# Sparse attention with two MLPs: thresholds moved to VectorE, v's product spread 2 and 3, the division in a job's fifth block

## The chip, the cores and the metric

The kernel runs on one core of a Trainium2 chip. The metric is the device time of one execution in microseconds, the median of three runs.

## The reference

Attention over 4 batches, 8 heads, 576 positions and 64 columns a head, followed by two MLPs over the 2304 tokens (512 to 2048 to 512 columns):

```python
scores = scale * np.matmul(q, k.transpose(0, 1, 3, 2))
thresh = np.max(scores, axis=-1, keepdims=True) - tau
scores = np.where(scores >= thresh, scores, -1000000000.0)
scores = scores - np.max(scores, axis=-1, keepdims=True)
attn = np.exp(scores)
attn = attn / (np.sum(attn, axis=-1, keepdims=True) + 1e-09)
attn_out = np.matmul(attn, v)
...
h = x @ w_in
g = np.where(h >= 1, h, np.where(h <= -1, 0.0, (h + 1) ** 2 / 4))
x = g @ w_out
...
h = x @ w_in
g = h * np.clip(h + 3.0, 0.0, 6.0) / 6.0
out = g @ w_out
```

All inputs and outputs are float32.

## The kernel before

The attention is cut into 16 jobs (a batch and a pair of heads), a job into five blocks of query rows: four of 128 rows for both heads, and a fifth that holds the last 64 rows of both. A block goes through these steps.

- Scores (`em_scores`, line 305): four matmuls on TensorE into the two halves of PSUM called P, one half for each head. A half is free again when its reader is done.
- Reduction (line 318): VectorE reads a head's scores, writes their negatives to `p` in SBUF and their row minimum to a column of `nm`. It is followed by a short readout of the accumulator.
- Exponential (`em_exp`, line 329): ScalarE makes `e` from `p` and `nm`, head by head.
- Threshold (line 333): GpSimd adds tau to both columns of `nm` at once and writes `th`.
- Mask (`em_mask`, line 339): VectorE compares `p` with `th`, multiplies by `e`, writes back to `p` and sums the rows into `z`.
- Transposes (`em_pt` and `em_tail`, line 263): TensorE turns `p`, one block later, four pieces for each head and one tail; ScalarE copies them to `Gf` and `Gt` (lines 363 and 377).
- The product with v (`pv_chunk`, line 399): each job has two groups of rows, a (blocks 1 and 2) and b (blocks 3 to 5), each of five chunks, a chunk being a matmul for each head.
- The division: `pre_norm` (lines 418, 419) adds 1e-9 to `z` and takes the reciprocal on VectorE, GpSimd spreads it (line 422), and `em_norm` (lines 436 to 445) transposes it on TensorE, multiplies on VectorE, stores x by SP's queue and starts loading v of the job after next.

`attention` writes this order down by hand, with a `yield` after each piece. Once the first four jobs are done, `mode["mlp"]` is set, and each `yield` gives the first MLP a credit of 0.57 pieces (`part1`, lines 602, 613 and 664), which take turns with the attention on TensorE. The weights of the MLPs are split into a high and a low part on ScalarE, VectorE and GpSimd (lines 116 to 142). A scheduler then sorts the instructions of each engine by its own simulated times and priorities, but within what `after` pins. `put` pins VectorE's attention work in the written order until `mode["mlp"]` is set.

In the attention alone a block has its products in two places, `pv_run(2)` after the first head's transposes and `pv_run(2)` at the end; beside the MLP it is `pv_run(3)` and `pv_run(2)`. There the division of a job stands in the third block of the next job; in the attention alone, in its fifth.

Of the kernel before, what the change touches and what calls it, by code (L numbers as in the profile page):

```python
# [18 lines left out]
def kernel(  # L19
# [185 lines left out]
    mode = {"mlp": False, "att": True, "step": False, "t": 0, "s": 0, "n": 0, "pin": True}  # L205
# [48 lines left out]
    last_on = {}  # L254

    def put(E, x):
        if mode["pin"] and E in "V":
            after(x, last_on.get(E))
        last_on[E] = x
        return x  # L260

    def turn(out, in_, pin):
        x = put("T", T.transpose(out, in_, ident))  # L263
        if pin:
            pe_pins.append(x)

    def unit_q(j):
        if j >= NJ or j in qt:
            return
        tm = unit_bank().rearrange("p e n -> p (e n)")  # L270
        for c in range(5):
            turn(tm[:, c * 128:(c + 1) * 128], qn[:, c, :], c == 0)
        load_q(j + 1)
        qt[j] = ap.tile([128, SEQ], F32, tag="qt", name="qt", bufs=2)
        reads(put("S", S.activation(out=qt[j], in_=tm[:, 0:SEQ], func=ACTF.Copy, scale=taus[:, 1:2])))

    def unit_k(j):

        if j >= NJ or j in kt:
            return  # L280
        tm = unit_bank().rearrange("p e n -> p (e n)")
        for i, c in enumerate((4, 0, 1, 2, 3, 4)):
            turn(tm[:, i * 128:(i + 1) * 128], kn[:, c, :], i == 0)
        load_k(j + 1)
        kt[j] = ap.tile([128, SEQ + TAIL], F32, tag="kt", name="kt", bufs=2)
        reads(put("S", S.activation(out=kt[j], in_=tm[:, 128 - TAIL:128 + MAIN + TAIL], func=ACTF.Copy)))
# [4 lines left out]
    def em_scores(j, i):  # L291

        last = i == NBLK - 1

        if not last:
            mode["s"] += 1
        ss = [unit_bank() for _ in range(1 if last else 2)]
        prev = None
        c = slice(i * 128, i * 128 + (TAIL if last else 128))
        for x, (h, e) in enumerate(((0, 0), (1, 1), (0, 1), (1, 0)) if last else ((0, 0), (1, 0), (0, 1), (1, 1))):  # L300
            r = slice(h * D, (h + 1) * D)
            k0 = e * HS + (TAIL if last or h == 0 else 0)
# [4 lines left out]
            prev = put("T", mm)  # L307
            if x == 0:
                pe_pins.append(mm)
                for y in range(1 if last else 2):  # L310
                    after(mm, readers.get((mode["s"] - y) % 2), True)
        nm = ap.tile([128, 2], F32, tag="nm", name="nm", bufs=3)
        th = ap.tile([128, 2], F32, tag="th", name="th", bufs=3)
        p = ap.tile([128, 2, 2, HS], F32, tag="p", name="p", bufs=3)
        if i == 0:
            zt[j] = ap.tile([128, 9], F32, tag="z", name="z", bufs=2)
        for x, s in enumerate(ss):
            reads(put("V", V.tensor_scalar(out=p[:, x], in0=s[:, :, 0:HS], scalar1=-1.0, scalar2=3e38,  # L318
                                           op0=ALU.mult, op1=ALU.min, accum_out=nm[:, x:x + 1])), len(ss) - 1 - x)
        blk[j, i] = (p, nm, th, [])  # L320
# [3 lines left out]
    def em_exp(j, i, x):  # L324
        p, nm, th, es = blk[j, i]
        if x >= (1 if i == NBLK - 1 else 2):
            return
        e = ap.tile([128, 2, HS], F32, tag="e", name="e", bufs=3)
        pins["S"] = put("S", S.activation(out=e, in_=p[:, x], func=ACTF.Exp, bias=nm[:, x:x + 1], scale=-1.0))  # L329
        es.append(e)  # L330
        if x == 0:
            n = 1 if i == NBLK - 1 else 2
            G.tensor_scalar(out=th[:, 0:n], in0=nm[:, 0:n], scalar1=taus[:, 0:1], scalar2=0.0, op0=ALU.add, op1=ALU.add)  # L333

    def em_mask(j, i):
        p, nm, th, es = blk.pop((j, i))
        for x, e in enumerate(es):
            z = ZCOL[x](i)
            put("V", V.scalar_tensor_tensor(out=p[:, x], in0=p[:, x], scalar=th[:, x:x + 1], in1=e,  # L339
                                            op0=ALU.is_le, op1=ALU.mult, accum_out=zt[j][:, z:z + 1]))  # L340
# [11 lines left out]
    def em_pt(j, i, h):  # L352
# [9 lines left out]
        if i < NBLK - 1:  # L362
            put("S", S.activation(out=f[:, h, :, d0:d0 + 128], in_=tm.rearrange("p (c n) -> p c n", c=4), func=ACTF.Copy))  # L363
        else:
            for x in HEADS:
                put("S", S.activation(out=f[:, x, :, d0:d0 + TAIL],
                                      in_=tm.rearrange("p (c h n) -> p h c n", c=4, h=2)[:, x], func=ACTF.Copy))

    def em_tail(j, i):
# [5 lines left out]
        if i < NBLK - 1:  # L375
            turn(tl[:, 0:128], p[:, MAIN:MAIN + 128], True)
            put("S", S.activation(out=t[:, d0:d0 + 128], in_=tl[:, 0:128], func=ACTF.Copy))
        else:
            turn(tl[0:TAIL, 0:128], p[:, MAIN:SEQ], True)
            for x in HEADS:  # L380
                put("S", S.activation(out=t[x * TAIL:(x + 1) * TAIL, d0:d0 + TAIL],
                                      in_=tl[0:TAIL, x * TAIL:(x + 1) * TAIL], func=ACTF.Copy))
# [3 lines left out]
    def pv_chunk():  # L386
# [10 lines left out]
        for h in (1, 0):  # L397
# [4 lines left out]
            prev = put("T", mm)  # L402
        if c == 4:
            del gt[g, j], o_t[j, g]
            put("S", S.activation(out=xu[j][:, d0:d0 + n], in_=o, func=ACTF.Copy))
# [7 lines left out]
    def pre_norm(j):  # L413
# [4 lines left out]
        put("V", V.tensor_scalar(out=z, in0=z, scalar1=1e-9, scalar2=None, op0=ALU.add))  # L418
        put("V", V.reciprocal(out=rz[:, :, 0], in_=z))
# [6 lines left out]
    def em_norm(j):  # L426
# [8 lines left out]
        for c in range(4):  # L435
            put("T", T.transpose(bm[:, c * 128:(c + 1) * 128], rb[:, c].rearrange("p h n -> p (h n)"), ident))
        bt = bm[:, 512:640]
        put("T", T.transpose(bt, rz[:, 4, :].to_broadcast([128, 128]), ident))
        x = xu.pop(j)
        put("V", V.tensor_tensor(out=x[:, 0:MAIN], in0=x[:, 0:MAIN], in1=bm[:, 0:MAIN], op=ALU.mult))  # L440
        if b < NB - 1:
            nc.sync.dma_start(out=xd[b][:, hp, :], in_=x[:, 0:MAIN])
        for h in HEADS:
            r = slice(64 * h, 64 * h + 64)
            reads(put("V", V.tensor_tensor(out=x[r, MAIN:SEQ], in0=x[r, MAIN:SEQ], in1=bt[r, 64 * h:64 * h + 64], op=ALU.mult)))
# [4 lines left out]
    def attention():  # L450
# [25 lines left out]
        for t in range(n + 6):  # L476
# [3 lines left out]
            if not mode["mlp"]:  # L480
                if t < n:
                    em_scores(j, i)
                    maskq.append((j, i))
                if t < n:
# [4 lines left out]
                yield  # L489
                now = due(1)  # L490
# [3 lines left out]
                pv_run(2)  # L494
                yield
# [4 lines left out]
                tails(1)  # L500
# [3 lines left out]
                pv_run(2)  # L504
# [12 lines left out]
            else:  # L517
# [24 lines left out]
                now = due(1)  # L542
# [319 lines left out]
    for _ in attention():  # L862
        if not mode["mlp"]:
# [9 lines left out]
            mode["pin"] = False  # L873
# [101 lines left out]
```

## Time and profile before

| | us |
|---|---|
| median of 3 runs | 1163.19 |
| lowest and highest | 1162.94 and 1165.3 |
| the profiled execution | 1165.27 |
| its span, first to last instruction | 1163.3 |

| engine | busy us | share of the span |
|---|---|---|
| TensorE (PE) | 1123.3 | 97% |
| VectorE (DVE) | 565.7 | 49% |
| ScalarE (ACT) | 627.6 | 54% |
| GpSimd (POOL) | 437.1 | 38% |

The shares are averages over stages that differ: the attention alone, the attention beside the MLP, and the two MLPs. The rows below are therefore taken by stage. A row of a group of instructions names the line, the engine, the operation, output and input; a row of the timeline begins with its start and its duration, and the bracket at its end tells how long the engine had been idle and what released it.

### The profile page before, as it was taken

Reading aid. Unit: us, or ns where it says so; the run is one execution under the profiler, and the core shown is the slowest. Engines: PE = TensorE matmul, PEld = TensorE weight load, DVE = VectorE, ACT = ScalarE, POOL = GpSimd, SP = SyncE. Lnnn points to the kernel's source line nnn. Section 1 sums busy time; section 2 is a strip of 40 time slices with the busy share of each in tenths; the row PEclk is TensorE's granted clock in tenths of the full one; section 3 lists DMA queues with packets and bytes.
Section 4 is the critical chain, followed back from the end, with each engine's and each line's share of the span. In section 5 each row is a group of like instructions: output and inputs, shape, how many; then the busy total and the mean of one; then the engine's idle time right before and its main releaser. Section 6 shows DMA issues by size and latency. Waiting matters only on the chain.

```text
span 1163.3 us, 17941 instructions
## 1 busy us (share of the span) xinstructions
PE 1123.3 (97%) x6680; PEld 900.7 (77%) x6680; DVE 565.7 (49%) x1128; ACT 627.6 (54%) x1234; POOL 437.1 (38%) x468
## 2 busy tenths in 40 slices
PE   7889888999999999999999999999999999999998
PEld 5455667677777777788889988888888888888886
DVE  4787886765564555624544756657631121121111
ACT  5676886766575656655665776645532222232222
POOL 1342675531121121215663765568722212222221
PEclk9999999999999999999999999999999999999999
DMA  6332434312112120002522345533110020010000
GB/s 165 89 89 61 119 93 134 103 50 69 37 47 52 43 52 22 11 11 92 154 73 89 106 142 156 179 109 109 55 59 1 1 68 1 1 46 1 19 1 37
DMA packets 105095, 79.82 MB, mean 69 GB/s; under 512 B 66352, under 2 KB 89904, under 8 KB 105008
## 3 DMA queue, kind: packets, MB, share of 16 engines
q1 hardware_dynamic: 103648, 78.38, 23.2%
q8 instruction: 53, 0.87, 0.3%
q10 hardware_dynamic: 1360, 0.30, 0.1%
q14 instruction: 34, 0.28, 0.1%
HBM read 61.34 MB, written 17.30 MB: 68 GB/s over the span
## 4 chain that ended last, share of the span: by engine, by line
PE 84%; DVE 8%; ACT 5%; issue 1%; POOL 1%; DMA 1%; ACTq 0%; DVEq 0%; POOLq 0%
PE Q L602 34%; PE P L644 27%; PE Q L664 7%; PE P L305 5%; PE Q L399 5%; PE Q L263 4%; DVE p L339 3%; DVE p L318 2%; ACT e L329 2%; ACT Gf L363 1%; PE P L263 1%; DVE w_c L133 1%; DVE xl L586 1%; DVE w_c L127 1%; POOL w_c L135 1%
## 5 line engine op out<-in xcount | busy, mean ns | idle before, releaser
L620 POOL TENSOR_TENSOR gl<-r,gh 128x512 fp32r<-128x512 f32 (+1 forms) x190 | 205.2, 1081 | 456.6 <-ACT gh L619 451.4
L602 PE MATMUL Q<-xh,wih 128*128 128x512 f32 (+1 forms) x760 | 264.4, 348 | 3.3 <-DVE r L613 3.2
L602 PE MATMUL Q<-xl,wih 128*128 128x512 f32 (+1 forms) x760 | 257.4, 339 | 0.0
L602 PE MATMUL Q<-xh,wil 128*128 128x512 f32 (+1 forms) x760 | 257.1, 338 | 0.0
L616 DVE SCALAR_TENSOR_TENSOR r<-r,Q 128x512 f32<-128x512 f32 (+1 forms) x80 | 50.7, 634 | 249.7 <-ACT r L615 249.6
L602 PEld LDWEIGHTS Q<-xh,wih 128*128 128x128 f32 x760 | 144.6, 190 | 33.7 <-issue 10.7
L619 ACT ACTIVATE gh<-r 128x512 fp32r<-128x512 f32 (+1 forms) x190 | 99.8, 526 | 122.1 <-PE P L644 52.7
L602 PEld LDWEIGHTS Q<-xl,wih 128*128 128x128 f32 x760 | 144.4, 190 | 16.1 <-issue 0.5
L602 PEld LDWEIGHTS Q<-xh,wil 128*128 128x128 f32 x760 | 144.2, 190 | 15.4
L339 DVE SCALAR_TENSOR_TENSOR p<-p,th,e 128x576 f32<-128x576 f32 x144 | 128.8, 911 | 42.4 <-POOL th L333 23.3
L318 DVE TENSOR_SCALAR_CACHE_REDUCE p<-P 128x576 f32<-128x576 f32 x144 | 103.6, 752 | 72.4 <-PE Q L263 50.8
L329 ACT ACTIVATE e<-p,nm 128x576 f32<-128x576 f32 x144 | 109.7, 774 | 49.5 <-DVE p L318 48.9
L615 ACT ACTIVATE r<-Q,three 128x512 f32<-128x512 f32 (+1 forms) x80 | 51.4, 643 | 144.2 <-PE Q L602 141.1
L263 PE MATMUL Q<-ident,p 128*128 128x128 f32 (+1 forms) x656 | 109.6, 282 | 16.1 <-DVE p L339 7.4
L613 DVE SCALAR_TENSOR_TENSOR r<-r,Q 128x256 f32<-128x256 f32 (+1 forms) x110 | 54.8, 499 | 121.9 <-ACT r L612 121.8
L263 PEld LDWEIGHTS Q<-ident,p 128*128 128x128 f32 (+1 forms) x656 | 72.8, 140 | 53.1 <-issue 12.2
L644 PE MATMUL P<-woh,gh 128*128 128x512 f32 x288 | 111.9, 390 | 0.6 <-DVE ob L702 0.6
L644 PE MATMUL P<-wol,gh 128*128 128x512 f32 x288 | 112.2, 390 | 0.0
L644 PE MATMUL P<-woh,gl 128*128 128x512 f32 x288 | 111.0, 390 | 0.0
L305 PE MATMUL P<-kt,qt 64*128 64x288 f32 (+1 forms) x640 | 99.2, 428 | 8.5 <-DVE p L318 6.7
L135 POOL TENSOR_TENSOR w_c<-w_c,w_raw 128x512 int32<-128x512 int32 x64 | 91.0, 1423 | 33.0 <-DVE w_c L133 23.9
L363 ACT ACTIVATE Gf<-Q 128x512 f32<-128x512 f32 x128 | 75.0, 591 | 39.7 <-PE Q L263 39.5
(85 smaller groups left out, 1873.5 us busy)
## 6 DMA issues: line engine op xcount, KB each, us to landing
w_raw<-in_moe_w_in_dram SPq DMA_DIRECT2D x32, 512.0 KB, 4.0
w_raw<-in_moe_w_out_dram SPq DMA_DIRECT2D x32, 512.0 KB, 3.7
kn<-in_k_dram SPq DMA_DIRECT2D x32, 128.0 KB, 2.6
vn<-in_v_dram SPq DMA_DIRECT2D x32, 128.0 KB, 2.8
x2p<-ob SPq DMA_DIRECT2D x16, 256.0 KB, 2.1
x2d<-ob SPq DMA_DIRECT2D x16, 256.0 KB, 3.5
xst<-x2d SPq DMA_DIRECT2D x16, 256.0 KB, 3.4
out_dram<-ob SPq DMA_DIRECT2D x16, 256.0 KB, 2.1
```

Of the source, the lines that this page charges most:

```text
L135: x = G.tensor_tensor(out=c.bitcast(I32), in0=c.bitcast(I32), in1=r, op=ALU.add)
L263: x = put("T", T.transpose(out, in_, ident))
L305: mm = T.matmul(o, qt[j][r, c], kt[j][r, k0:k0 + HS], start=True, stop=True, skip_group_check=True)
L318: reads(put("V", V.tensor_scalar(out=p[:, x], in0=s[:, :, 0:HS], scalar1=-1.0, scalar2=3e38, op0=ALU.mult, op1=ALU.min, accum_out=nm[:, x: ...
L329: pins["S"] = put("S", S.activation(out=e, in_=p[:, x], func=ACTF.Exp, bias=nm[:, x:x + 1], scale=-1.0))
L339: put("V", V.scalar_tensor_tensor(out=p[:, x], in0=p[:, x], scalar=th[:, x:x + 1], in1=e, op0=ALU.is_le, op1=ALU.mult, accum_out=zt[j][:, ...
L363: put("S", S.activation(out=f[:, h, :, d0:d0 + 128], in_=tm.rearrange("p (c n) -> p c n", c=4), func=ACTF.Copy))
L602: mm = T.matmul(h, l[:, kk * 128:(kk + 1) * 128], r, start=(x == 0), stop=(x == 3 * KD - 1))
L619: x = S.activation(out=gh, in_=r, func=ACTF.Copy)
L620: y = G.tensor_tensor(out=gl, in0=r, in1=f32(gh), op=ALU.subtract)
L644: T.matmul(a, l, r, start=(first and x == 0), stop=(last and x == 2))
L664: mm = T.matmul(o, l, r, start=(f == fs[0] and x == 0 and i == 0), stop=(f == fs[-1] and x == 2 and i == 1), skip_group_check=True)
```

## The change

The threshold becomes one small addition for each head, on VectorE instead of GpSimd. `put` and the pins of VectorE's order go. In the attention alone the products come as `pv_run(2)` right behind the scores and `pv_run(3)` at the end, the tail is turned ahead of the heads, and `pre_norm` stands between the two heads' transposes. Beside the MLP they come as `pv_run(2)` twice, `pre_norm` comes right behind the masks, and the division moves from the third block to the fifth. Where a `put(...)` is merely taken away, the diff is left out.

```diff
@@ em_exp
-        if x == 0:
-            n = 1 if i == NBLK - 1 else 2
-            G.tensor_scalar(out=th[:, 0:n], in0=nm[:, 0:n], scalar1=taus[:, 0:1], scalar2=0.0, op0=ALU.add, op1=ALU.add)
+        V.tensor_scalar(out=th[:, x:x + 1], in0=nm[:, x:x + 1], scalar1=taus[:, 0:1], scalar2=None, op0=ALU.add)
...
-    last_on = {}
-
-    def put(E, x):
-        if mode["pin"] and E in "V":
-            after(x, last_on.get(E))
-        last_on[E] = x
-        return x
...
@@ attention, alone
                     em_scores(j, i)
                     maskq.append((j, i))
+                pv_run(2)
+                yield
                 if t < n:
                     em_exp(j, i, 0)
                 if t < n:
                     em_exp(j, i, 1)
                 blocks_of("m", lag=0 if t < n else 0)
                 yield
+                tails(1)
                 now = due(1)
                 for b in now:
                     em_pt(*b, 0)
                     yield
-                pv_run(2)
-                yield
+                if i == 0 and 0 < j <= NJ:
+                    pre_norm(j - 1)
                 for b in now:
                     if b[1] < NBLK - 1:
                         em_pt(*b, 1)
                         yield
-                tails(1)
                 for b in now:
                     if b[1] in AFTER:
                         pvq.extend((b[0], AFTER[b[1]], c) for c in range(5))
-                pv_run(2)
+                pv_run(3)
+                if i == 4:
+                    unit_k(j + 1)
+                    yield
                 if i == 3:
                     unit_q(j + 1)
                     yield
-                if i == 4:
-                    unit_k(j + 1)
-                    yield
-                if i == 0 and 0 < j <= NJ:
-                    pre_norm(j - 1)
...
@@ attention, beside the MLP
                 blocks_of("m", lag=0 if t < n else 0)
+                if i == 0 and 0 < j <= NJ:
+                    pre_norm(j - 1)
                 yield
                 tails(2)
-                pv_run(3)
+                pv_run(2)
                 yield
-                if i == 0 and 0 < j <= NJ:
-                    pre_norm(j - 1)
-                if i == 2 and 0 < j <= NJ:
+                now = due(1)
+                if i == 4 and 0 < j <= NJ:
                     em_norm(j - 1)
                     done_jobs.add(j - 1)
                     yield
...
-                now = due(1)
```

The order of VectorE (DVE) in the first job, its third and fourth blocks (lines 318 and 310 are the reductions, 339 and 329 the masks, 323 the new thresholds). Before:

```order
L318 TENSOR_SCALAR p,nm<-P_239 128x576
L318 TENSOR_SCALAR p,nm<-P_240 128x576
L339 SCALAR_TENSOR_TENSOR p,z<-p,th,e 128x576 x2
L318 TENSOR_SCALAR p,nm<-P_288 128x576
L318 TENSOR_SCALAR p,nm<-P_289 128x576
L339 SCALAR_TENSOR_TENSOR p,z<-p,th,e 128x576 x2
```

With the change:

```order
L310 TENSOR_SCALAR p,nm<-P_241 128x576
L310 TENSOR_SCALAR p,nm<-P_242 128x576
L323 TENSOR_SCALAR th<-nm,taus 128x1 x2
L329 SCALAR_TENSOR_TENSOR p,z<-p,th,e 128x576
L310 TENSOR_SCALAR p,nm<-P_293 128x576
L329 SCALAR_TENSOR_TENSOR p,z<-p,th,e 128x576
L310 TENSOR_SCALAR p,nm<-P_294 128x576
L323 TENSOR_SCALAR th<-nm,taus 128x1 x2
L329 SCALAR_TENSOR_TENSOR p,z<-p,th,e 128x576 x2
```

The thresholds stand behind the reductions, and the fourth block's first reduction stands between the third block's two masks.

The order of TensorE (PE) in the third job's first two blocks (305 and 297 are the scores, 399 and 389 the products with v of the second job, 263 and 255 the transposes of p). Before, from the first block's last score on:

```order
L305 MATMUL P_640<-kt,qt 128x288
L399 MATMUL Q_675<-Gf,vn_97 64x320 x4
L305 MATMUL P_686<-kt,qt 128x288
L305 MATMUL P_687<-kt,qt 128x288
L305 MATMUL P_686<-kt,qt 128x288
L305 MATMUL P_687<-kt,qt 128x288
L263 MATMUL Q_706<-ident,p 128x128 x4
L399 MATMUL Q_675<-Gf,vn_97 64x320 x4
L263 MATMUL Q_716<-ident,p 128x128 x4
L263 MATMUL Q_722<-ident,p 128x128
L399 MATMUL Q_675<-Gt,vn_97 64x320 x2
```

With the change:

```order
L297 MATMUL P_648<-kt,qt 128x288
L389 MATMUL Q_690<-Gf,vn_97 64x320 x6
L297 MATMUL P_697<-kt,qt 128x288
L297 MATMUL P_698<-kt,qt 128x288
L297 MATMUL P_697<-kt,qt 128x288
L297 MATMUL P_698<-kt,qt 128x288
L389 MATMUL Q_690<-Gf,vn_97 64x320 x2
L389 MATMUL Q_690<-Gt,vn_97 64x320 x2
L255 MATMUL Q_726<-ident,p 128x128 x4
L255 MATMUL Q_723<-ident,p 128x128
L255 MATMUL Q_732<-ident,p 128x128 x4
```

Six products instead of four lie between the two blocks' scores, and the other four stand together ahead of the transposes; the tail stands between the two heads.

## Rows read from the trace of the kernel before

**Rows 1.** Busy time by stage: stretch, length, busy us (count) by engine, PEclk, DMA.

```profile
6.20:118.40 112.20, 96.51 (x672) 58.40 (x672) 82.26 (x210) 75.63 (x155) 32.45 (x53) 0.98 0.39 102
118.40:240.00 121.60, 107.33 (x770) 81.78 (x770) 95.63 (x200) 93.80 (x202) 76.44 (x85) 0.97 0.37 105
240.00:521.00 281.00, 277.38 (x2096) 216.38 (x2095) 148.56 (x392) 173.42 (x382) 51.81 (x96) 1.00 0.16 41
...
82.00:100.00 18.00, 14.59 (x102) 9.22 (x104) 13.87 (x32) 11.66 (x27) 9.23 (x10) 0.95 0.36 97
```

**Rows 2.** Waits of TensorE, 6.2 to 118.4: us in total, times, longest.

```profile
PE Q L263 <- DVE p L339: 7.4, 6, 1.6
PE P L305 <- DVE p L318: 5.8, 10, 1.5
```

**Rows 3.** Waits of VectorE, 6.2 to 118.4.

```profile
DVE p L339 <- POOL th L333: 10.6, 19, 1.3
...
DVE p L339 <- ACT e L329: 7.0, 9, 1.2
```

**Rows 4.** Timeline, 53 to 72 us: start, duration, instruction, idle time before it.

```profile
53.33 1.45 ACT L329 ACTIVATE e<-p,nm 128x576 f32<-128x576 f32 x2 [1.59 <-DVE p L318]
...
54.84 1.80 DVE L339 SCALAR_TENSOR_TENSOR p<-p,th,e 128x576 f32<-128x576 f32 x1 [0.93 <-POOL th L333]
...
58.26 0.75 DVE L318 TENSOR_SCALAR_CACHE_REDUCE p<-P 128x576 f32<-128x576 f32 x1
58.44 0.78 ACT L329 ACTIVATE e<-p,nm 128x576 f32<-128x576 f32 x1 [3.66 <-DVE p L318]
...
59.12 0.30 POOL L333 TENSOR_SCALAR th<-nm,taus 128x2 f32<-128x2 f32 x1 [0.46 <-DVE p L318]
...
59.45 0.82 DVE L339 SCALAR_TENSOR_TENSOR p<-p,th,e 128x576 f32<-128x576 f32 x1 [0.43 <-POOL th L333]
59.60 0.76 ACT L329 ACTIVATE e<-p,nm 128x576 f32<-128x576 f32 x1
...
60.39 0.82 DVE L339 SCALAR_TENSOR_TENSOR p<-p,th,e 128x576 f32<-128x576 f32 x1
...
70.73 0.77 ACT L329 ACTIVATE e<-p,nm 128x576 f32<-128x576 f32 x1
...
71.36 0.31 POOL L333 TENSOR_SCALAR th<-nm,taus 128x1 f32<-128x1 f32 x1
...
71.70 1.80 DVE L339 SCALAR_TENSOR_TENSOR p<-p,th,e 128x576 f32<-128x576 f32 x1 [1.27 <-POOL th L333]
```

**Rows 5.** Small additions on VectorE: timeline at the start, line 418's durations, its group.

```profile
3.73 0.15 DVE L818 TENSOR_SCALAR taus<-taus 128x1 f32<-128x1 f32 x1 [3.73 <-DMA taus<-in_tau_dram]
3.80 0.14 DVE L819 TENSOR_SCALAR taus<-taus 128x1 f32<-128x1 f32 x1
...
L418 DVE TENSOR_SCALAR z<-z x16: 158/172/1154, 33.9 to 499.6; 128x9 f32<-128x9 f32 x16
...
L418 DVE TENSOR_SCALAR z<-z 128x9 f32<-128x9 f32 x16 | 5.1, 318 | 0.3
```

**Rows 6.** Timeline of TensorE: scores, four products, nine transposes.

```profile
50.66 1.24 PE L305 MATMUL P<-kt,qt 64*128 64x288 f32 x8 [0.29 <-ACT kt L286]
...
51.83 1.30 PE L399 MATMUL Q<-Gf,vn 128*64 128x320 f32 x8
...
61.07 1.20 PE L263 MATMUL Q<-ident,p 128*128 128x128 f32 x9
```

**Rows 7.** 118.4 to 240: waits of masks for thresholds; busy time of the scores.

```profile
DVE p L339 <- POOL th L333: 2.0, 4, 0.6
...
118.40:240.00 121.60, 20.85 (x136) 11.06 (x136) 0.97 0.37 105
```

**Rows 8.** Timeline at 147 us: GpSimd and line 418.

```profile
146.70 1.82 POOL L135 TENSOR_TENSOR w_c<-w_c,w_raw 128x512 int32<-128x512 int32 x1
...
147.40 1.15 DVE L418 TENSOR_SCALAR z<-z 128x9 f32<-128x9 f32 x1
```

More of the change, by code (lines that the diff above doesn't have):

```diff
@@ L252, in reads @@
         readers[(mode["s"] - ago) % 2] = x
-    last_on = {}
-    def put(E, x):
-        if mode["pin"] and E in "V":
-            after(x, last_on.get(E))
-        last_on[E] = x
-        return x
     def turn(out, in_, pin):
-        x = put("T", T.transpose(out, in_, ident))
+        x = T.transpose(out, in_, ident)
         if pin:
@@ L274, in unit_q @@
         qt[j] = ap.tile([128, SEQ], F32, tag="qt", name="qt", bufs=2)
-        reads(put("S", S.activation(out=qt[j], in_=tm[:, 0:SEQ], func=ACTF.Copy, scale=taus[:, 1:2])))
+        reads(S.activation(out=qt[j], in_=tm[:, 0:SEQ], func=ACTF.Copy, scale=taus[:, 1:2]))
     def unit_k(j):
@@ L285, in unit_k @@
         kt[j] = ap.tile([128, SEQ + TAIL], F32, tag="kt", name="kt", bufs=2)
-        reads(put("S", S.activation(out=kt[j], in_=tm[:, 128 - TAIL:128 + MAIN + TAIL], func=ACTF.Copy)))
+        reads(S.activation(out=kt[j], in_=tm[:, 128 - TAIL:128 + MAIN + TAIL], func=ACTF.Copy))
     zt, gt, xu, p_t = {}, {}, {}, {}
@@ L306, in em_scores @@
             after(mm, prev)
-            prev = put("T", mm)
+            prev = mm
             if x == 0:
@@ L338, in em_mask @@
             z = ZCOL[x](i)
-            put("V", V.scalar_tensor_tensor(out=p[:, x], in0=p[:, x], scalar=th[:, x:x + 1], in1=e,
-                                            op0=ALU.is_le, op1=ALU.mult, accum_out=zt[j][:, z:z + 1]))
+            V.scalar_tensor_tensor(out=p[:, x], in0=p[:, x], scalar=th[:, x:x + 1], in1=e,
+                                            op0=ALU.is_le, op1=ALU.mult, accum_out=zt[j][:, z:z + 1])
         p_t[j, i] = p.rearrange("p h e n -> p (h e n)")
@@ L376, in em_tail @@
             turn(tl[:, 0:128], p[:, MAIN:MAIN + 128], True)
-            put("S", S.activation(out=t[:, d0:d0 + 128], in_=tl[:, 0:128], func=ACTF.Copy))
+            S.activation(out=t[:, d0:d0 + 128], in_=tl[:, 0:128], func=ACTF.Copy)
         else:
@@ L380, in em_tail @@
             for x in HEADS:
-                put("S", S.activation(out=t[x * TAIL:(x + 1) * TAIL, d0:d0 + TAIL],
-                                      in_=tl[0:TAIL, x * TAIL:(x + 1) * TAIL], func=ACTF.Copy))
+                S.activation(out=t[x * TAIL:(x + 1) * TAIL, d0:d0 + TAIL],
+                                      in_=tl[0:TAIL, x * TAIL:(x + 1) * TAIL], func=ACTF.Copy)
     o_t, pvq = {}, []
@@ L401, in pv_chunk @@
             after(mm, pe_pins[-1] if h else prev)
-            prev = put("T", mm)
+            prev = mm
         if c == 4:
             del gt[g, j], o_t[j, g]
-            put("S", S.activation(out=xu[j][:, d0:d0 + n], in_=o, func=ACTF.Copy))
+            S.activation(out=xu[j][:, d0:d0 + n], in_=o, func=ACTF.Copy)
     def pv_run(n):
@@ L417, in pre_norm @@
         rz = ap.tile([128, 9, 1], F32, tag="rz", name="rz", bufs=2)
-        put("V", V.tensor_scalar(out=z, in0=z, scalar1=1e-9, scalar2=None, op0=ALU.add))
-        put("V", V.reciprocal(out=rz[:, :, 0], in_=z))
+        V.tensor_scalar(out=z, in0=z, scalar1=1e-9, scalar2=None, op0=ALU.add)
+        V.reciprocal(out=rz[:, :, 0], in_=z)
         rb = ap.tile([128, 4, 2, 64], F32, tag="rb", name="rb")
@@ L444, in em_norm @@
             r = slice(64 * h, 64 * h + 64)
-            reads(put("V", V.tensor_tensor(out=x[r, MAIN:SEQ], in0=x[r, MAIN:SEQ], in1=bt[r, 64 * h:64 * h + 64], op=ALU.mult)))
+            reads(V.tensor_tensor(out=x[r, MAIN:SEQ], in0=x[r, MAIN:SEQ], in1=bt[r, 64 * h:64 * h + 64], op=ALU.mult))
         nc.sync.dma_start(out=xd[NB][:, hp, b * TAIL:(b + 1) * TAIL], in_=x[:, MAIN:SEQ])
```

21 lines of the change are left out of this document (10 added, 11 removed).

## The prediction

> **What bounds the kernel now.** I began with the busy times by stage [rows 1]. The reader should see three stages ahead of the pure MLP work. The attention alone (6.2 to 118.4 us) keeps TensorE busy 96.5 of 112.2 us. The attention beside the first weight splitting (118.4 to 240) keeps it busy 107.3 of 121.6. The rest of the attention (to 521) leaves 281.0 - 277.4 = 3.6 us idle, and after it come only the MLPs. The changed kernel issues the same matmuls, so it can only move idle time, 15.7 us in the first stage and 14.3 in the second, or the clock. [...]
>
> Then the waits of the first stage. TensorE waited 7.4 us for masks (line 339), 6 times, and 5.8 us for reductions (line 318), 10 times: 13.2 of its 15.7 us, on 16 occasions [rows 2]. The stage holds 25 blocks (five jobs, since the MLP begins when the first four are done, in the fifth job's last block), so VectorE's chain (reduction, threshold and exponential, mask) ends last in about 16 of 25. On VectorE the masks waited 10.6 us for GpSimd's threshold, 19 times, and 7.0 us for the exponential, 9 times [rows 3].
>
> **Thresholds on VectorE.** An ordinary block shows what the move is worth [rows 4]. The second reduction starts at 58.26 and takes 0.75, so it ends near 59.01. GpSimd's threshold runs from 59.12 to 59.42, and the mask starts at 59.45. The first head's exponential ran from 58.44 to 59.22. Without GpSimd the mask can start near 59.25. It gains 0.2 us and no more, because the exponential comes next. The same holds where GpSimd's queue made the wait long, at 71.70: the threshold ended at 71.67, the exponential at 71.50. Only at 54.84 was the exponential long done (two from 53.33 on in 1.45, the first by about 54.1), and there 0.7 us go. Together 18 x 0.2 + 0.7 = 4.3 us of VectorE's time.
>
> What it adds: no row has this operation inside a block. The nearest are two 128x1 operations at the start, 0.15 us long and 0.07 apart [rows 5], so a pair takes 0.07 + 0.15 = 0.22 us. It fits into the 0.2 us in which VectorE waits for the exponential anyway, which is its cover. With that cover gone it would cost 25 x 0.22 = 5.5 us in this stage, more than is saved. An addition on 128x9 has a median of 0.172 us but once took 1.154, and that dear end is taken up under the rivals. TensorE gets its share of what VectorE saves: 4.3 x 16/25 = **2.8 us**, between 0 and 4.3; I take it because the 128x1 rows are nearest in shape and they are short.
>
> **Nothing pinned.** In the new order 10 of the stage's 20 two-headed blocks have the next block's first reduction between their two masks (before, none). Where the second mask would wait for its exponential (7.0 / 9 = 0.78 us a time, in 9 of 20 blocks), the reduction fills the wait: 10 x 9/20 x 0.78 x 16/25 = 2.2 us at most. Against it, the second mask comes 0.83 us later (a reduction and a readout), and TensorE waited for a mask in 6 of 25 blocks: 10 x 6/25 x 0.83 = 2.0 us lost. I take **0**, between -2.0 and +2.2.
>
> **The products of v.** Four products take 1.30 us, a block's scores 1.24, its nine transposes 1.20 [rows 6]. In a job's first block TensorE has 1.24 + 1.30 = 2.5 us to do, in the second 1.24 + 6/4 x 1.30 + 1.20 = 4.4. VectorE's two reductions and two masks take 2 x 0.75 + 2 x 0.82 = 3.1 us and the waits. So the first block is VectorE's and the second TensorE's. In jobs 2, 3 and 4 one chunk (two products, 0.65 us) moves from the second to the first, which gains 3 x 0.65 = 1.95 us. In job 1 the opposite happens: all ten products lie in the second block, four more than before, which costs 1.30. Sum **0.65 us**, between -1.3 (the cost alone) and +2.0 (the gain alone). In the fourth blocks ten products now stand in a row between the transposes of the two heads. The next scores come no later by that, since the same ten lay in that block before.
>
> **The clock.** The dip costs 0.05 x 18.0 = 0.9 us [rows 1]. If the stops around it shrink it may go, if they grow there may be another. I take half, **0.45 us**, between -0.9 and +0.9.
>
> **The later stages.** From 118.4 to 240 there are 17 blocks (136 score records, 8 a block), and masks waited only 2.0 us for thresholds [rows 7]. VectorE, busy 95.6 of 121.6 us, gets 17 x 0.22 = 3.7 us more, and GpSimd, busy 76.4, loses its thresholds. I count 0, between +2.0 (those waits) and -3.7 (VectorE last throughout). The division moves to a job's fifth block, two blocks later, with its five transposes and three multiplications, which meet the transposes of k there. The MLP needs job 7's result after 240 products of line 602. The new order has exactly 240 ahead of that division (before, 228), so almost nothing queues behind it: 0. Were the MLP held up for the two blocks in each of the two batches that still follow, these four blocks would run as in the first stage, which idles 15.7 / 25 = 0.63 us a block: 2.5 us. On SP's queue the stores of x go out two blocks later, and so does v's next load, which is still several blocks ahead of its first use: 0. Past 240 us TensorE has 3.6 us idle to give, and a longer VectorE chain is covered by MLP matmuls: 0.
>
> **Sum.** 2.8 + 0 + 0.65 + 0.45 = 3.9 us. The profiled execution took 1165.27 us (its span is 1163.3), 2.08 above the median of 1163.19. Its own time becomes 1161.4, and the median, rounded, **1159** us.
>
> **Rivals.**
> *Slower: the threshold is caught behind GpSimd.* At 147.40 the 128x9 addition on VectorE took 1.15 us, while GpSimd's operation begun at 146.70 ran 1.82, to 148.52 [rows 8]. Both ended together. The addition's 16 cases average 0.318 us against the median of 0.172, so 0.146 more [rows 5]. If each block's pair pays that and the masks gain nothing, 25 + 17 blocks up to 240 us cost 42 x 0.146 = 6.1 us: **1169**. It decides from the point where a pair costs more than the 0.2 us of its cover. For it speaks that GpSimd is busy 76.4 of 121.6 us in the second stage. Against it, that the mask behind the threshold is caught by such operations already (1.80 instead of 0.82 at 54.84), so most of this wait is not new. Chance 0.20.
>
> [...]
>
> *No change.* The waits for the threshold become waits for the exponential, which queues on ScalarE behind the copies. In the block of rows 4 the second mask started at 60.39, just when its exponential (59.60 and 0.76) ended, and would do so again. Then the block's start moves but not its end, and the time stays at **1163**, within 2.3 us. Chance 0.24. That the change does nothing at all is excluded by the order, which moves all three engines' work.
>
> *More.* With all terms of the first stage at their upper ends, 4.3 + 2.2 + 2.0 + 0.9 = 9.4 us, and 2.0 from the second: 1163.2 - 11.4, or **1152**. [...] Chance 0.16.
>
> **How the numbers follow.** The forecast, from 1154 to 1160.9, has the remaining 0.40. A measurement of this kernel can tell about 0.2%, or 2.3 us, from no change. Faster: 0.40 + 0.16 = 0.56. Same: 0.24. Slower: 0.20. The range runs from all upper ends, 1152, to 1167, where two thirds of the slower case's price have been paid; what that case costs beyond, and the little below 1152, are under 0.2 together.
>
> **What would show it.** Right: no wait of a mask for GpSimd; waits for the exponential above 7.0 us; the first 25 blocks done about 4 us before 118.4; TensorE's idle time there near 12 us; thresholds near 0.15 us each. Wrong: thresholds of up to a microsecond, waits for masks above 7.4 us, TensorE idle well over 14.3 us in the second stage, or the lower clock in more stretches than before.

## The result, and the profile after

The changed kernel takes 1149.03 us (median of 4 runs, 1147.81 to 1149.29), the kernel before 1163.21 beside it: a ratio of 0.9872 (0.9855 to 0.9889). That is 14.2 us less where 4 were forecast, and 3 us below the range. The profiled executions are 17.3 us of span apart (1163.3 and 1146.0), since that of before lies 2.1 us above its median and that of after 1.2 below.

By stage, after (columns as in [rows 1]), with the stage of the MLPs alone as a fourth:

```profile
6.20:110.40 104.20, 91.19 (x676) 60.01 (x677) 87.93 (x257) 77.15 (x156) 24.70 (x28) 1.00 0.42 111
110.40:232.00 121.60, 112.35 (x826) 84.22 (x825) 104.23 (x245) 97.62 (x212) 71.16 (x71) 1.00 0.39 109
232.00:503.00 271.00, 270.07 (x2034) 208.44 (x2033) 147.92 (x444) 167.41 (x369) 37.55 (x55) 1.00 0.16 41
503.00:1146.00 643.00, 638.59 (x3133) 541.10 (x3132) 236.57 (x327) 283.37 (x498) 275.45 (x221) 1.00 0.22 68
```

The attention beside the MLP as one stretch, and what follows it, before:

```profile
118.40:520.40 402.00, 384.11 (x2859) 297.56 (x2860) 243.59 (x590) 266.61 (x581) 128.25 (x181) 0.99 0.22 60
...
520.40:1163.30 642.90, 638.62 (x3134) 541.01 (x3132) 239.60 (x328) 284.01 (x499) 274.75 (x221) 1.00 0.22 68
```

The attention alone is 8.0 us shorter (112.2 to 104.2), the attention beside the MLP 9.4 (402.0 to 121.6 + 271.0 = 392.6), the rest is unchanged. In the first stage TensorE's idle time fell by 2.7 us (15.7 to 13.0) and its busy time by 5.3. Beside the MLP idle time fell from 17.9 to 10.2 and busy time by 1.7. Much of the gain is thus busy time, which the prediction held to be fixed.

The waits of TensorE in the first stage, after, answer to [rows 2]:

```profile
PE P L297 <- DVE p L310: 5.4, 9, 1.5
PE Q L255 <- DVE p L329: 3.5, 4, 1.7
```

Those of VectorE there answer to [rows 3]:

```profile
DVE p L310 <- PE P L297: 10.6, 11, 4.1
DVE p L329 <- ACT e L321: 4.0, 7, 0.8
```

The threshold wait is gone (10.6 us before), waits for the exponential fell too (7.0 to 4.0), and the masks that TensorE waits for cost 3.5 us instead of 7.4. The new thresholds, and below them the 128x9 addition, after (minimum, median and longest in ns):

```profile
L323 DVE TENSOR_SCALAR th<-nm,taus x144: 199/207/216, 12.0 to 479.8; 128x1 f32<-128x1 f32 x144
...
L408 DVE TENSOR_SCALAR z<-z x16: 165/173/1164, 28.0 to 481.4; 128x9 f32<-128x9 f32 x16
```

Not one of the 144 thresholds was held up behind GpSimd, while the 128x9 addition still was, up to 1.16 us. In 19 of the 144 cases an operation of GpSimd that had begun earlier was still running, as here:

```profile
63.88 1.28 POOL L142 TENSOR_TENSOR wil<-w_c,wih 128x512 fp32r<-128x512 f32 x1
...
63.93 0.33 DVE L323 TENSOR_SCALAR th<-nm,taus 128x1 f32<-128x1 f32 x2
```

The pair ends 0.90 us ahead of GpSimd's operation.

Busy time of v's products, before, in the two stages (TensorE first; a product leaves two records, so eight records are four products):

```profile
6.20:118.40 112.20, 28.38 (x180) 10.78 (x180) 0.98 0.39 102
118.40:520.40 402.00, 66.20 (x460) 28.94 (x460) 0.99 0.22 60
```

and after:

```profile
6.20:110.40 104.20, 24.20 (x180) 11.85 (x180) 1.00 0.42 111
110.40:503.00 392.60, 71.05 (x460) 26.95 (x460) 1.00 0.23 62
```

The same matmuls cost 4.2 us less in the first stage and 4.85 more beside the MLP. What differs is the number of separate runs (products that follow each other without another kind of matmul between them), counted in TensorE's order: 27 runs of products before and 12 after in the first stage, 46 and 68 beside the MLP. Beside the MLP 4.85 / 22 = 0.22 us a run. In the first stage 15 runs make 3.3 us of the 4.2; the rest is a fall of the clock (below), in which eight records took 2.16 us instead of 1.30:

```profile
99.82 2.16 PE L399 MATMUL Q<-Gf,vn 128*64 128x320 f32 x8
```

The trace of before has the cost of a run already, in two lengths of one shape:

```profile
42.11 1.08 PE L399 MATMUL Q<-Gf,vn 128*64 128x256 f32 x8
43.81 0.65 PE L399 MATMUL Q<-Gt,vn 128*64 128x256 f32 x4
```

Eight records take 1.08 us and four 0.65, so a run costs 2 x 0.65 - 1.08 = 0.22 us over and above its records. A little of it lies under the start of the next matmul: from start to start (the next begin at 43.12 and 44.40) it is 2 x 0.59 - 1.01 = 0.17.

The granted clock (last column but two) in those stretches of 4 us in which it fell, TensorE alone, before:

```profile
98.00:102.00 4.00, 4.00 (x18) 0.57 0.84 247
150.00:154.00 4.00, 1.84 (x11) 0.85 0.36 118
154.00:158.00 4.00, 3.73 (x24) 0.72 0.46 131
178.00:182.00 4.00, 1.21 (x6) 0.76 0.62 182
182.00:186.00 4.00, 4.00 (x30) 0.81 0.37 88
```

There are three falls (the last four rows are two of them), each worth the same 4 x 0.43 = 1.7 us of clock. After, no stretch of 4 us up to 240 us shows one. What a fall looks like on TensorE's timeline, before (waits in brackets):

```profile
149.76 0.66 PE L263 MATMUL Q<-ident,p 128*128 128x128 f32 x4
152.58 0.41 PE L602 MATMUL Q<-xh,wih 128*128 128x256 f32 x1 [2.16 <-DVE r L613]
152.80 0.40 PE L602 MATMUL Q<-xl,wih 128*128 128x256 f32 x1
```

After a stop of 2.16 us the MLP's matmuls start 0.21 us apart, where they otherwise start 0.12 apart. The granted clock was 0.50 there from 153.0 to 156.0 us, against 1.00 up to 152.5 and from 156.5 on.

TensorE's longest waits beside the MLP, before:

```profile
PE P L263 <- DVE p L318: 4.0, 2, 2.8
PE Q L602 <- DVE r L613: 3.2, 5, 2.2
```

and after:

```profile
PE Q L592 <- DVE r L603: 2.8, 4, 1.4
PE P L255 <- DVE p L310: 1.4, 1, 1.4
```

The two stops of over 2 us, one ahead of each of the two falls there, are gone; the longest is now 1.4 us.

### The profile page after: what moved, and what is told of

Its sections match the earlier page's. It is cut to its first block, busy times and chain, and to the rows that moved or that the text cites. A ratio compares the mean times of both kernels' runs of the same rounds, so it can differ in the third digit from the quotient of the medians.

```text
span 1146.0 us, 18037 instructions
## 1 busy us (share of the span) xinstructions
PE 1116.3 (97%) x6680; PEld 897.5 (78%) x6680; DVE 576.9 (50%) x1272; ACT 626.9 (55%) x1234; POOL 410.5 (36%) x388
## 4 chain that ended last, share of the span: by engine, by line
PE 86%; DVE 6%; ACT 4%; issue 1%; DMA 1%; POOL 1%; ACTq 0%; DVEq 0%; POOLq 0%
PE Q L592 34%; PE P L634 27%; PE Q L654 7%; PE P L297 6%; PE Q L389 6%; PE Q L255 5%; DVE p L310 2%; DVE p L329 2%; ACT e L321 1%; PE P L255 1%; ACT Gf L353 1%; DVE xl L576 1%; DVE w_c L133 0%; DMA w_raw<-in_moe_w_in_dram 0%; PE P L426 0%
## 5 line engine op out<-in xcount | busy, mean ns | idle before, releaser
L592 PEld LDWEIGHTS Q<-xh,wil 128*128 128x128 f32 x760 | 143.6, 189 | 15.2
L310 DVE TENSOR_SCALAR_CACHE_REDUCE p<-P 128x576 f32<-128x576 f32 x144 | 104.3, 753 | 58.8 <-PE Q L255 46.2
L634 PE MATMUL P<-wol,gh 128*128 128x512 f32 x288 | 112.2, 390 | 0.0
L135 POOL TENSOR_TENSOR w_c<-w_c,w_raw 128x512 int32<-128x512 int32 x64 | 87.5, 1368 | 42.1 <-DVE w_c L133 34.4
```

Source lines behind the costliest of these rows:

```text
L135: x = G.tensor_tensor(out=c.bitcast(I32), in0=c.bitcast(I32), in1=r, op=ALU.add)
L310: reads(V.tensor_scalar(out=p[:, x], in0=s[:, :, 0:HS], scalar1=-1.0, scalar2=3e38, op0=ALU.mult, op1=ALU.min, accum_out=nm[:, x:x + 1]), ...
L592: mm = T.matmul(h, l[:, kk * 128:(kk + 1) * 128], r, start=(x == 0), stop=(x == 3 * KD - 1))
L634: T.matmul(a, l, r, start=(first and x == 0), stop=(last and x == 2))
```

## The experiments

The ratio is against the kernel before on the same chip. Differences in us in the text are of medians, against 1149.0 unless another is named; from chip to chip the medians of one kernel differ by 1 to 2 us (1163.2 to 1165.4 for the kernel before, 1149.0 and 1147.9 for the changed one), so differences of 2 to 3 us rest on the profiles and not on the medians alone. The stages are the attention alone, and from there to the MLPs alone. "Falls" counts falls of the clock in the profiled execution.

| kernel | median us | ratio (95% interval) | attention alone: us, idle | beside MLP: us, idle | falls |
|---|---|---|---|---|---|
| before | 1163.2 | 1 | 112.2, 15.7 | 402.0, 17.9 | 3 |
| changed | 1149.0 | 0.987 (0.986 to 0.989) | 104.2, 13.0 | 392.6, 10.2 | 0 |
| changed, again | 1147.9 | 0.984 (0.982 to 0.986) | 105.4, 12.6 | 393.1, 10.8 | 1 |
| u_th | 1155.9 | 0.992 (0.990 to 0.995) | 110.4, 17.2 | 397.1, 11.6 | 3 |
| a_th | 1156.7 | 0.993 (0.992 to 0.995) | 107.0, 11.4 | 398.0, 15.6 | 1 |
| v_th2 | 1152.8 | 0.990 (0.988 to 0.991) | 109.6, 15.9 | 393.4, 11.0 | 1 |
| u_pin | 1151.5 | 0.988 (0.984 to 0.993) | not read | 393.0, 10.2 | 1 |
| u_alone | 1151.8 | 0.988 (0.984 to 0.992) | 108.0, 14.0 | 392.4, 10.0 | 0 |
| v_single | 1158.4 | 0.995 (0.993 to 0.996) | 114.8, 16.2 | 392.5, 10.2 | 0 |
| w_a05 | 1152.2 | 0.988 (0.986 to 0.990) | 108.3, 16.5 | 392.8, 10.0 | 0 |
| w_a50 | 1153.3 | 0.989 (0.987 to 0.991) | 109.8, 17.2 | 392.2, 9.9 | 1 |
| w_05 | 1152.1 | 0.989 (0.988 to 0.991) | 105.4, 12.7 | 395.7, 20.4 | 3 |
| u_norm | 1155.4 | 0.992 (0.990 to 0.994) | 104.3, 12.9 | 399.3, 12.9 | 1 |
| u_mlp | 1158.0 | 0.994 (0.991 to 0.996) | 104.0, 12.9 | 402.6, 16.2 | 3 |
| w_32 | 1157.8 | 0.994 (0.992 to 0.996) | 106.8, 12.7 | 401.1, 19.7 | 3 |
| a_norm5 | 1161.3 | 0.997 (0.996 to 0.998) | 112.2, 15.7 | 397.6, 15.7 | 4 |
| a_pv22 | 1164.3 | 0.999 (0.998 to 1.000) | 112.8, 13.8 | 400.6, 12.4 | 5 |
| a_mlp | 1159.7 | 0.996 (0.994 to 0.997) | 113.7, 14.0 | 394.5, 11.5 | 3 |

### The thresholds

u_th puts GpSimd's threshold back into the changed kernel, a_th puts VectorE's into the kernel before and changes nothing else (its order stays pinned):

```diff
-        V.tensor_scalar(out=th[:, x:x + 1], in0=nm[:, x:x + 1], ...)
+        if x == 0:
+            G.tensor_scalar(out=th[:, 0:n], in0=nm[:, 0:n], ...)
```

> The changed kernel with one part undone: the thresholds of both heads in one GpSimd operation, as before. Theory 'waits' (the thresholds' move carries the gain, as my prediction's largest term had it): 1149 rises by 5 to 8 us, and masks wait about 10 us for thresholds again ahead of the MLP. Theory 'runs' (the gain of the first stage is that v's products stand in longer runs): it rises by at most 3 us, and the stage ahead of the MLP stays within 2 us of 110.4.

> The kernel before with the thresholds alone on VectorE, head by head, in the pinned order. If the move is worth by itself what undoing it cost (7 us): 1156, the first stage 6 us shorter. If it only pays with the order free: 1160 to 1163, with waits for the exponential where those for the threshold were.

The first stage of u_th:

```profile
6.20:116.60 110.40, 93.22 (x676) 60.38 (x677) 81.39 (x212) 77.23 (x156) 31.47 (x53) 0.98 0.40 105
```

and of a_th:

```profile
6.20:113.20 107.00, 95.57 (x672) 59.11 (x672) 85.21 (x255) 75.84 (x156) 24.79 (x28) 0.98 0.41 107
```

Undone, idle time there rises from 13.0 to 17.2 us, and the masks wait 11.1 us for thresholds again, 19 times. Done alone, it falls from 15.7 to 11.4. Both are 4.2 to 4.3 us. The stretch beside the MLP moves as well: 4.5 us longer in u_th (397.1 against 392.6, two falls more) and 4.0 shorter in a_th (398.0 against 402.0, two falls fewer). The time follows: 6.9 us more, and 0.7% less, as the first theory of each had it. The threshold alone is thus worth about half of the 14.2 us, and about half of that lies beside the MLP.

v_th2 makes one operation of VectorE for both heads in the changed kernel:

```diff
-        V.tensor_scalar(out=th[:, x:x + 1], in0=nm[:, x:x + 1], ...)
+        if x == 0:
+            V.tensor_scalar(out=th[:, 0:n], in0=nm[:, 0:n], ...)
```

> The changed kernel with one threshold operation on VectorE for both heads (128x2) in place of one for each (128x1). If an operation of more than one column is caught behind GpSimd as the 128x9 addition was (1.15 us), thresholds of up to 1 us show in the second stage and the time rises by 2 to 6 us, to 1151 to 1155. If not, a threshold takes about 0.21 us throughout, but it waits for the second head's reduction, and the time is 1147 to 1150.

Its thresholds, all and by shape (busy us, mean ns):

```profile
L333 DVE TENSOR_SCALAR th<-nm,taus x80: 202/228/1140, 12.6 to 486.0; 128x2 f32<-128x2 f32 x64, 128x1 f32<-128x1 f32 x16
...
L333 DVE TENSOR_SCALAR th<-nm,taus 128x2 f32<-128x2 f32 x64 | 19.2, 299 | 1.7
```

and one case, with GpSimd beside it:

```profile
133.99 1.27 POOL L142 TENSOR_TENSOR wol<-w_c,woh 128x512 fp32r<-128x512 f32 x1
...
134.29 0.99 DVE L333 TENSOR_SCALAR th<-nm,taus 128x2 f32<-128x2 f32 x1
```

Both end within 0.02 us of each other. The 128x2 operation is held up behind GpSimd in 10 of 64 cases (longest 1.14 us, mean 0.30 against a median of 0.23). These are the 10 in which an operation of GpSimd that had begun earlier was still running, and each ended 0.02 to 0.03 us after it. The 128x1 operation met such an operation 19 times in the changed kernel and was never held up. The longest of its 144 took 0.216 us. Why two columns are held up beside GpSimd and one is not was not shown.

The 1152.8 us lie in the first theory's range, but not by its account. The 3.7 us that v_th2 loses to the changed kernel lie in the first stage (109.6 us, against 105.4 where the changed kernel had one fall of the clock too) and not beside the MLP (393.4 against 392.6 and 393.1). Its 20 pairs of the first stage take no more VectorE time than single operations do (20 x 0.320 = 6.4 us, against 6.9 for the changed kernel's 20 pairs of single ones, which take 0.33 to 0.34 us a pair). What is left as a cause is that the first head's mask has to wait for the second head's reduction, and that the cases held up come at a bad moment; the two were not told apart. TensorE waits 5.6 us for masks there instead of 3.5.

### The pins

u_pin pins VectorE's order in the changed kernel as before:

```diff
-    mode = {..., "n": 0}
+    mode = {..., "n": 0, "pin": True}
```

> The changed kernel with VectorE's pins back in the attention alone, thresholds included in the pinned order. Theory 'waits': up by 2 to 4 us, masks wait longer for the exponential. Theory 'runs': within 2 us of 1149.

1151.5 us, 2.5 more, as the first theory had it. But that is little more than chips differ by, and the interval of its ratio (0.984 to 0.993) holds the changed kernel's 0.987, so it doesn't settle between the two. Its profiled execution took 1156.3, 4.8 above its own median: from 6.2 to 20 us TensorE was busy for 11.13 us with 45 records, where the changed kernel has 9.86 us with 68, at a granted clock of 1.00 in both. What made those records longer was not shown, so its first stage isn't read.

### The order of the products in the attention alone

u_alone gives the changed kernel the old order there. v_single places the chunks one by one, 39 runs instead of 12. w_a05 and w_a50 put all five at the end of a block, or behind its scores, 9 runs:

```diff
-                pv_run(2)
+                pv_run(0)
...
-                pv_run(3)
+                pv_run(5)
```

(w_a05; w_a50 has 5 and 0.)

> The changed kernel with the written order of the attention alone as before (products 2 and 2, tail behind the heads, pre_norm late). Theory 'runs': TensorE's busy time in v's products ahead of the MLP goes from 24.2 back to about 28.4 us, the stage is 4 to 6 us longer and the time near 1154. Theory 'waits': within 2 us of 1149.

> The changed kernel with v's chunks spread one by one over each block of the attention alone: 39 runs of products on TensorE ahead of the MLP in place of 12 (27 before the change). Theory 'runs' (each run costs some 0.22 us more, the difference between four products at 0.76 us and twice the half of eight at 1.30): TensorE's busy time in them rises from 24.2 to about 30 us, the stage from 104.2 to 107 or more, the time to 1152 or more. If the length of the runs costs nothing: 24 us, 104, 1149.

> The changed kernel with all five chunks of v's products at the end of a block in the attention alone, 9 runs of products there instead of 12. If a run's fixed cost is all that counts, the first stage is 3 x 0.22 = 0.7 us shorter: 1147.5 to 1149.5. If ten products in a row make the next block's scores late, it is 1150 to 1153.

> The changed kernel with all five chunks of v's products right behind a block's scores in the attention alone, again 9 runs instead of 12. If a run's fixed cost is all that counts: 1147.5 to 1149.5. If ten products in a row make the transposes and so the copies late, 1150 to 1153.

Products of v_single in the first stage:

```profile
6.20:121.00 114.80, 30.16 (x180) 9.43 (x180) 1.00 0.39 101
```

and of w_a05:

```profile
6.20:114.50 108.30, 23.55 (x180) 12.13 (x180) 1.00 0.40 106
```

For 39, 23 (u_alone), 12 and 9 runs the products take 30.16, 26.63, 24.20 and 23.55 us, none of them with a fall of the clock: 0.22 us a run throughout. u_alone's 108.0 us are 3.8 more than the changed kernel's, 2.4 of them this cost; its time lies between its two theories. v_single's stage is 10.6 us longer, where the first theory had 2.8 or more: 6.0 of that is this cost, and 3.2 is idle time. But the fewest runs are not the fastest. What TensorE waited for in the first stage of w_a05:

```profile
PE Q L263 <- DVE p L337: 7.6, 8, 1.7
PE P L305 <- DVE p L318: 5.5, 8, 1.5
```

and of w_a50:

```profile
PE P L305 <- DVE p L318: 11.1, 11, 2.3
PE Q L263 <- DVE p L337: 3.5, 5, 1.7
```

With all products at the end TensorE waits 7.6 us for masks (3.5 in the changed kernel). With all of them behind the scores it waits 11.1 us for reductions (5.4). Both are 4 to 5 us slower than the changed kernel on the same chip, near the second theory of each, so two and three chunks are a spread that covers both waits. The late copies that w_a50's theory named are not among its long waits.

### Beside the MLP

u_mlp gives the changed kernel the whole old order beside the MLP, u_norm only the division's old place, w_32 only three chunks at the first place again. a_mlp, a_norm5 and a_pv22 put all of it, the division alone, and the products with the reciprocal alone, into the kernel before. w_05 puts all five chunks at the second place (24 runs).

```diff
@@ u_norm
-                if i == 4 and 0 < j <= NJ:
+                if i == 2 and 0 < j <= NJ:
                     em_norm(j - 1)
@@ w_32 (w_05: 0 here, and 5 for the second pv_run(2))
                 tails(2)
-                pv_run(2)
+                pv_run(3)
```

> The changed kernel with the written order beside the MLP as before (products 3 and 2, division in the third block). If the 9 us that the trace shows gained after the MLP's start come from this order: near 1157, with TensorE idle 12 us or more between the MLP's start and 240 us. If they come from the thresholds leaving GpSimd there, or only from what the first stage hands over: within 3 us of 1149.

> The changed kernel with one thing undone, the division beside the MLP: in a job's third block again, the products staying at 2 and 2. If the division's place carries the 9 us that the order beside the MLP is worth: near 1158, with the stage from the MLP's first matmul to the wide matmuls near 402 us. If the products' 2 and 2 (and pre_norm's place) carry it: near 1149 and 393 us.

> The kernel before with the new order beside the MLP alone; thresholds on GpSimd, pins and the first stage as before. If that order pays by itself: 1163 falls to 1153 to 1156, the stage beside the MLP from 402 to about 393 us. If it pays only together with thresholds on VectorE (the run with thresholds back on GpSimd had 397): about 1158. The first stage stays at 112 us in any case.

> The changed kernel with three chunks of products at a block's first place beside the MLP instead of two (46 runs instead of 68), and the division left in the fifth block. If the division's place is what mattered beside the MLP, the time is that of the changed kernel or up to 5 us less (22 runs x 0.22): 1144 to 1150. If the products' even spread mattered, it lies between the changed kernel and the one whose whole order beside the MLP is the old one (1158): 1152 to 1156.

> The kernel before with one thing changed, the division in a job's fifth block beside the MLP instead of the third. If the place of the division is a gain of its own, as its undoing in the changed kernel suggests (6.3 us), the time is 1156 to 1159, and the stretch from the first MLP product to the wide ones falls from 402.0 to about 396 us. If it only works together with the spread of the products, the time is within 2 us of 1163.

> The kernel before with v's products beside the MLP in two and two chunks and the reciprocal right behind the masks, the division still in the third block. If the spread of the products is a gain of its own, idle time of TensorE past the weight splitting falls from 3.6 to about 1 us, the 22 more runs cost 22 x 0.22 = 4.8 us of busy time, and the sum is 1160 to 1164. If the two edits beside the MLP only work together, it is 1162 to 1165, with as many stretches at the lower clock as before.

> The changed kernel with v's products beside the MLP in one piece: all five chunks at a block's second place, none at the first, so that there are 24 separate runs of products on TensorE instead of 68. The theory that each run of products has a fixed cost of 0.22 us (four products 0.76, eight 1.30) says that the products beside the MLP take 71.05 - 44 x 0.22 = 61.4 us of TensorE, and the time falls by 4 to 10 us, to 1139 to 1145. The rival that spreading the products is what keeps the MLP and the softmax apart says that ten products in a row let the masks and scores come late: TensorE idle above 10.1 us there, and the time between 1149 and 1156.

In the changed kernel either half undone loses most of the gain: 6.3 us for the division, 8.8 for the products, 9.0 for both. There the halves need each other. Put into the kernel before, the division alone gains 0.3%, the products alone nothing that can be told from none, both 0.4%: there they merely add up, to less than the 9.0 us. So single effects put into the kernel before are no guide to what the same edits are worth in the changed one.

u_mlp came out as its first theory had it, with 12.6 us idle up to 240 us. u_norm, at 1155.4 us, lies between its two. a_mlp came out near its second in time, but its stage beside the MLP is 7.5 us shorter, near the first; its first stage, which should have stayed, has three falls instead of one. a_norm5 lies just inside its second theory's range, though its 0.3% is clear of no change. a_pv22 lies in its second theory's range. w_32 fell outside the 1144 to 1156 us of both its theories.

One stop shows how they mesh. u_norm at 140 us, TensorE:

```profile
140.31 0.28 PE L662 MATMUL Q<-gl,woh 128*128 128x256 f32 x1
143.58 0.58 PE L662 MATMUL Q<-gh,wol 128*128 128x256 f32 x1 [3.00 <-POOL wol L142]
```

and GpSimd ahead of that:

```profile
141.12 1.01 POOL L420 TENSOR_SCALAR rb<-rz 128x256 f32<-128x256 f32 x2
142.11 1.42 POOL L142 TENSOR_TENSOR wol<-w_c,woh 128x512 fp32r<-128x512 f32 x1
```

The changed kernel at the same place, TensorE:

```profile
140.93 0.28 PE L654 MATMUL Q<-gl,woh 128*128 128x256 f32 x1
142.20 1.24 PE L297 MATMUL P<-kt,qt 64*128 64x288 f32 x8 [0.99 <-DVE p L310]
143.37 0.66 PE L255 MATMUL Q<-ident,p 128*128 128x128 f32 x4
143.78 0.36 PE L654 MATMUL Q<-gh,wol 128*128 128x256 f32 x1
```

and GpSimd there:

```profile
142.08 1.54 POOL L142 TENSOR_TENSOR wol<-w_c,woh 128x512 fp32r<-128x512 f32 x1
```

In both GpSimd delivers the split weight at about 143.6 (142.11 + 1.42 and 142.08 + 1.54). In u_norm TensorE's next instruction is the one that needs it, and it stops for 3.0 us, after which the clock falls (0.70 granted from 142 to 146 us; the matmul behind it takes 0.58 us instead of 0.36). In the changed kernel a block's scores and four transposes stand ahead of it, and only 0.99 us are lost at this place.

w_05's stretch beside the MLP, and its products:

```profile
111.60:507.30 395.70, 375.26 (x2857) 297.93 (x2856) 253.84 (x688) 264.64 (x580) 110.47 (x126) 0.99 0.22 61
...
111.60:507.30 395.70, 61.34 (x460) 30.91 (x460) 0.99 0.22 61
```

The second theory's range holds. The 44 runs fewer save 71.05 - 61.34 = 9.7 us of TensorE's time, just as worked out, and idle time grows from 10.2 to 20.4. Nothing is left of it: here runs were not worth merging, since waits stood behind them.

### The changed kernel again

after_2 is the changed kernel on another chip.

> The changed kernel itself once more, beside which the next two are to be compared: 1147.8 to 1151, and no stretch at the lower clock if its shorter stops are the cause, one or two if the clock falls by chance.

1147.9 us, with one fall. Its stretch at the lower clock:

```profile
50.00:54.00 4.00, 4.00 (x20) 0.57 0.60 212
```

The stop ahead of it, before the transposes at 48.66, is 1.68 us long; the same stop is 1.69 in the first profile, where no fall followed, and in both TensorE was busy 6.06 of the 8 us up to 50. So the length of a stop does not by itself decide whether a fall follows. This one cost 105.4 - 104.2 = 1.2 us of the stage.

None of these kernels is faster than the changed one.

## Why the prediction was wrong

*The sign and the first cause were right.* Thresholds on VectorE shorten its chain. What mis-sized the term is the share: "TensorE gets its share of what VectorE saves: 4.3 x 16/25 = 2.8". The whole 4.3 us came off TensorE's idle time in a_th, and 4.2 came back in u_th, so nothing was lost in the 9 blocks that the prediction left out. (That VectorE's saving had been put at just 4.3 is in part luck: it was worked out from three cases.) The products also merged from 27 runs to 23 in a_th, another 0.9 us, which with 4.3 is the 5.2 us by which its stage is shorter.

*The slower rival* (thresholds caught behind GpSimd) fell by 144 durations of 0.199 to 0.216 us. The row that it was built on has nine columns; v_th2 shows that two columns are enough to be caught and one is not. The threshold itself cost 0.207, not the 0.15 of the nearest rows, and a pair 0.33 to 0.34, not 0.22. That is more than the 0.2 us of cover from which the prediction let this rival win, and yet TensorE's idle time fell.

*Nothing pinned*, counted as 0 between -2.0 and 2.2: 2.5 us undone, a little above its upper end, but not clear of what chips differ by. The prediction counted 10 blocks with a reduction between their two masks; VectorE's order in the first stage has it in 5 of the 20, one a job, so both its bounds were twice too wide. That the reduction fills the wait for the exponential agrees with the 4.0 us left of 7.0. The prediction named "waits for the exponential above 7.0 us" as the sign of being right, and that was wrong: it held for VectorE's old order only (7.9 us in a_th).

*The products of v*, 0.65: the step that moved chunks between blocks left out what a run costs, and halved the 1.30 us of two chunks to 0.65 for one, where the trace has 0.76 for one alone. The 15 runs fewer are 15 x 0.22 = 3.3 us of the 5.3 by which TensorE was busy less. u_alone puts the new order at 3.8 us in the stage, 2.8 in the medians.

*The clock*, 0.45: the prediction looked for falls in the first stage only, found one and took half. But [rows 1] showed the other two: 0.97 over 121.6 us is 3.6 us of clock. All three are gone in the changed kernel's profile. At 1.2 us (the changed kernel's two profiles) to 1.7 us each they are 3.6 to 5.1 us. The two stops of over 2 us ahead of the falls beside the MLP are gone as well. That these stops were the cause fits u_norm, where a stop of 3.0 us came back and a fall behind it, but it was not tested apart from the rest, in after_2 a fall followed a stop of 1.68 us, behind which the first profile has none, and in a_th a stop as long was followed by none:

```profile
176.83 0.39 PE L662 MATMUL Q<-gh,woh 128*128 128x256 f32 x1 [2.13 <-DVE ob L675]
```

One profile is also a poor count. For every execution the mean granted clock was taken, and a fall is 1.7 / 1150 = 0.0015 of it. The profiled execution of the changed kernel, at 1.000, is the highest of its four, the other three at 0.997 and 0.998; this explains why it lies below its median and, in part, why the profiles are further apart than the medians. Over all executions the changed kernel has 0.9988 (8 of them) and the kernel before 0.9954 (53), about 2.3 falls fewer. That they go with the order beside the MLP is shown by u_mlp, where all eight executions are back at 0.993 to 0.996, and that they go with the thresholds too by a_th, at 0.996 to 0.999.

*The later stages*, 0: this is the step that failed by most. "Past 240 us TensorE has 3.6 us idle to give" and the 14.3 before that were seen, but the terms there came to nothing: the thresholds at 0 (between +2.0 and -3.7), the division at 0 (at worst 2.5 us lost), and none was made for v's products in two and two. The runs showed instead that the stretch beside the MLP is 9.4 us shorter, with 7.7 of its 17.9 us of idle time gone. The thresholds alone are worth 4.0 us there (a_th), and the order beside the MLP 9.0 us when undone.

*The sum* by stages then reads: in the first, 2.7 us of idle time, 3.3 of runs and 1.2 to 1.7 of clock make 7.2 to 7.7 of 8.0. Beside the MLP, 7.7 of idle time and 2.4 to 3.4 of clock, less 4.85 for 22 more runs, make 5.3 to 6.3 of 9.4. The other 3 to 4 us are busy time of other matmuls there, the same ones that the two falls had stretched: by line 108.6 and 105.8 us for the MLP's first products (602), 101.1 and 99.9 for its second (664), 94.4 and 92.0 for the transposes (263). The falls aren't all of it, since a_th, without a fall there, still has 106.9, 100.4 and 93.0. What shortened them further was not found. Nor was it settled why the division's new place brings nothing in the changed kernel while the products stand three and two (w_32 against u_mlp).

## What to carry to other kernels

Count the separate runs of each kind of matmul in the new order, not only the matmuls, and take a run's fixed cost from two lengths of one shape; then check that no wait stands behind a run that is merged. Read the granted clock in windows of a few microseconds over the whole trace before any edit is called neutral, since the two stops of over 2 us beside the MLP and the two falls behind them went together here; and compare its mean over all executions, since one profile may be the one without a fall. Where an engine stops for a late operand, look at how much other work the new order puts ahead of it (in the one stop followed here it made 2 us), and this is a matter of all the edits together, so test them undone from the whole as well as one by one.

## What was not expected of the hardware

- One column more can make an addition on VectorE wait for GpSimd: 128x1 took at most 0.216 us in 144 cases, 19 of them beside an operation of GpSimd already running; 128x2 was held up in all 10 of its 64 cases beside one, up to 1.14 us.
- A run of v's products costs 0.22 us of TensorE's busy time over and above its matmuls, the same from 9 runs to 39 and in both stages.
- Falls of the clock come in one size, 1.7 us of clock each, in every profile here, from none to five of them (a_pv22), and the same stop of 1.7 us was followed by one in one execution and not in another. A stop of 2.13 us was followed by none.
